# Routing words in cluster-major order, a pairwise maximum, and a DMA transpose in a fused attention and convolution kernel

## The chip, the cores and the metric

The kernel runs on one core of a Trainium2 chip. The engines that matter are TensorE (PE, matmul), VectorE (DVE), ScalarE (ACT), GpSimd (POOL) and SyncE (SP, which here only issues DMAs). The metric is the device time of one launch in microseconds; it is given as the median of several runs. Engines run side by side, each in its own instruction order, and wait for one another by semaphores.

## The reference

Every query and every key is assigned to one of 16 clusters (the first centroid of largest cosine), and a query attends only to keys of its own cluster. The attention output then goes through a gated long convolution.

```python
q_assign = np.argmax(np.einsum('bhsd,hcd->bhsc', q_n, c_n), axis=-1)
k_assign = np.argmax(np.einsum('bhsd,hcd->bhsc', k_n, c_n), axis=-1)
mask = q_assign[:, :, :, None] == k_assign[:, :, None, :]
scores = scale * np.matmul(q, k.transpose(0, 1, 3, 2))
scores = np.where(mask, scores, -1000000000.0)
...
proj = x @ w_proj
...
x2_conv = np.fft.irfft(X2 * H, n=S, axis=1)
y = x1 * x2_conv * x3
return (y @ w_out).astype(np.float32)
```

Sizes: batch 4, 8 heads, 768 tokens, head size 64, 16 clusters, model width 512.

## The kernel before

**Tiling.** The 32 heads are worked in eight groups (`n` = 0 to 7) of four heads; a group has two pairs of heads (`pr` = 0, 1). `attention(n, pr)` makes six steps over blocks of 128 keys. A step is three score products of 512 columns (L662, recorded as L70 or L72), three exponentials on ACT (L671, L674), one product with the values (L685) and a running sum of the exponentials on DVE (L699). After every second group `hyena(b)` adds the convolution of one batch element as filler work.

**The mask.** Cluster membership is not a separate step of the scores: it is 16 more rows of the contraction. The tile `aug` holds 64 rows of the head and 16 rows with a word for every token. For a key (`j` = 1) the word is one-hot; for a query (`j` = 0) it is 0 at its cluster and a large negative number elsewhere, so that a key of another cluster gets a score that the exponential turns to 0. There are three sets of `aug` tiles, used in turn (`ring`).

**Routing.** `routing(n)` makes these words for a whole group (4 heads, each with queries and keys, `z` counts pair and query/key). For groups 1 to 7 it goes so:

1. `sim` (L582): similarities of all tokens to the centroids on PE; copied out by ACT or DVE; transposed by PE (`simT`, L595), so that tokens lie on the 128 partitions and each partition has 48 words of 16 numbers.
2. DVE: the maximum of each word (L602), twice (two halves); a comparison with it (L604), twice. A word can now have several ones.
3. DVE: a product with the descending numbers `revc` (L607), a second maximum over all 48 words (L610) and a second comparison (L612), which leaves the first one of each word.
4. PE: six transposes of 128x128 back to words on partitions, each in two halves (`ohT`, L623), into a PSUM bank; ACT (or DVE) copies the bank to the tile `ohT` with a scale and an offset per partition, which makes the query's form of the word (L629, L631).
5. SP: eight small DMAs per group (`masks`, L459) carry 16 rows of `ohT` each to the `aug` tiles: first the four of `pr` = 0, then the four of `pr` = 1.

Group 0 has a path of its own (`first_masks`), pair by pair.

**Order.** `build` lists all operations with a cost per engine that may take them, and a due time. `Plan.place` is a list scheduler: at each step it takes, on the engine that comes free first, the operation of the smallest due time among those that are ready, with a few terms added: `bonus` favours staying with value products on PE, `shape` speaks against changing the width of the PE array, `BUSY` speaks against giving DVE an operation that another engine could take, `LEAD` is how far ahead of its due time a load may be issued. A DMA's landing is planned from its bytes, a rate and a constant (`done`). The result is one fixed instruction order for each engine. Due times hang on `A(i)`, the planned time of attention step `i` (`T0`, `TAU1` for the first 28 steps, `TAU2` after); the mask words of a group are due relative to `b0`, a fixed time ahead of the group's first score.

Of the kernel before, what the change touches and what calls it, by code (L numbers as in the profile page):

```python
# [32 lines left out]
NV = 3  # L33
NU = 4
ROWS = 16
LEAD = 0.305
FIRST = 2
BUSY = 1.562
HELD = 4
THIRDS = [[(0, 0, 512)], [(0, 512, 768), (1, 0, 256)], [(1, 256, 768)]]  # L40
HOLD = {"score": "score", "o": "o"}
# [33 lines left out]
class Plan:  # L75
# [31 lines left out]
        self.ops.append(o)  # L107
        return o

    def place(self, free0, banks_for, switch=0.1, wait=0.1, rate=215e3, bonus=8.964, margin=0.036, shape=2.605):  # L110
        free = dict(free0)
        bank_free = [0.0] * 8
        ready = {e: [] for e in free}
# [57 lines left out]
        while any(ready.values()):  # L171
            best = None
            for e, lst in ready.items():
                f = free[e]
                cand = []
                for o in lst:
                    t = max(f, o.ready)
# [22 lines left out]
            _, e, o, t = best  # L200
# [40 lines left out]
def build(T):  # L241

    P = Plan()
    op = P.op
    T0 = 12.859
    TAU1 = 3.281
    TAU2 = 3.567
    NE = 28

    def ring(n, pr):  # L250
# [2 lines left out]
    def A(i):  # L253
        return T0 + TAU1 * min(i, NE) + TAU2 * max(i - NE, 0)

# [8 lines left out]
    def ap(h):  # L264
        return bank(h.ids[0])

    def bank(i):
        return T.bank[i][:]
# [7 lines left out]
    def dma(e):  # L276
        return (T.nc.scalar if e == "ACT" else T.nc.sync).dma_start
# [174 lines left out]
    def masks(n, prs, due):  # L452
        out = []
        for pr in prs:
            a = ring(n, pr)
            for hp in range(2):
                for j in (1, 0):
                    r0 = 32 * (2 * pr + j) + 16 * hp
                    out.append(op(("SP", .6), lambda e, a=a, hp=hp, j=j, r0=r0: dma(e)(  # L459
                        T.augs[a][hp][j][64 - 64 * hp:80 - 64 * hp], T.ohT[r0:r0 + 16]), due + .3 * hp,  # L460
                        r=[("ohT", pr), ("zero", a, j)], w=[("augm", a, hp, j)], byts=25e3, lat=1.0))
        return out

# [70 lines left out]
    def routing(n):  # L534
# [38 lines left out]
                       w=[("aug", ring(n, pr), hp, j)], lock=True)  # L573
        if n == 0:
            return got + first_masks(1)
        b0 = end - 21.084
        h = Bank(cls, 2)

        def sim(e, h=h):
            for ch in range(2):  # L580
                for z in range(4):
                    T.nc.tensor.matmul(bank(h.ids[ch])[32 * z:32 * z + 32, :384], T.cbd[:, 2 * g + z // 2],  # L582
                                       T.qkT[z][:, ch], start=True, stop=True)
        op(("PE", 1.33), sim, b0, r=[("qkT", z, ch) for z in range(4) for ch in range(2)] + ["cbd"], w=[h], alloc=h,
           kind="sim")
# [12 lines left out]
        bc = lambda a: a.unsqueeze(len(a.shape)).to_broadcast([*a.shape, NC])  # L598
        flat = lambda: T.oh[:].rearrange("p a n c -> p (a n) c")
        for ch in range(2):  # L600
            sv = lambda ch=ch, h=h: bank(h.ids[ch])[:, :384].rearrange("p (n c) -> p n c", c=NC)
            op(("DVE", .55), lambda e, ch=ch, sv=sv: V().tensor_reduce(T.mx[:, ch], sv(), axis=AX, op=Alu.max),  # L602
               b0 + 3.3 + .2 * ch, r=[h], w=[("mx", ch)])
            op(("DVE", .55), lambda e, ch=ch, sv=sv: V().tensor_tensor(T.oh[:, ch], sv(), bc(T.mx[:, ch]),  # L604
                                                                       op=Alu.is_equal),
               b0 + 3.4 + .2 * ch, r=[h, ("mx", ch)], w=[("oh", ch)], free=[h])
        op(("DVE", .56), lambda e: V().tensor_tensor(  # L607
            flat(), flat(), T.revc[:].unsqueeze(1).to_broadcast([128, 48, NC]), op=Alu.mult), b0 + 4, r=["revc"],
           w=both("oh"), lock=True)
        op(("DVE", .96), lambda e: V().tensor_reduce(T.m2, T.oh, axis=AX, op=Alu.max), b0 + 4.1, r=both("oh"),  # L610
           w=both("m2"))
        op(("DVE", .97), lambda e: V().tensor_tensor(T.oh, T.oh, bc(T.m2[:]), op=Alu.is_equal), b0 + 4.2,  # L612
           r=both("m2"), w=both("oh"), lock=True)
        h = Bank(cls)
        due = b0 + 7.5

        def ohT(e, h=h):
            o = ap(h).bitcast(BF16)
            f = T.oh[:].rearrange("p a n c -> p (a n c)")
            for t in range(NT):  # L620
                for i in range(1 if T.whole else 2):
                    rs = slice(0, 128) if T.whole else slice(64 * i, 64 * i + 64)
                    T.nc.tensor.transpose(o[rs, ts(t, 128)], f[:, ts(t, 128)][:, rs], T.identb)  # L623
        op(("PE", .335), ohT, due, r=[("oh", 0), ("oh", 1), "identb"], w=[h], alloc=h, kind="proj")

        def rows(e, h=h):
            x = ap(h).bitcast(BF16)[:, :S]
            if e == "ACT":
                T.nc.scalar.activation(T.ohT, x, Act.Identity, scale=T.mka, bias=T.mkb)  # L629
            else:  # L630
                T.nc.vector.tensor_scalar(T.ohT, x, T.mka, T.mkb, op0=Alu.mult, op1=Alu.add)  # L631
        op({"ACT": .83, "DVE": .68}, rows, due + .5,
           r=[h, "mk"], w=[("ohT", 0), ("ohT", 1)], free=[h])
        masks(n, range(2), due + 1.3)


# [308 lines left out]
    def constants():  # L945
        G = lambda: T.nc.gpsimd

        def ident(e):
            make_identity(T.nc, T.ident)
        op(("POOL", 1.0), ident, 0, w=["ident"])  # L950

        def iotas(e):
            kw = dict(allow_small_or_imprecise_dtypes=True)
            G().iota(T.s0t, pattern=[[2, 3]], base=0, channel_multiplier=6, **kw)
            for i in range(2):
                G().iota(T.kc[:, i], pattern=[[2, 192]], base=i, channel_multiplier=0, **kw)
            G().memset(T.kc[:, 0, 0:1], float(HS))
        op(("POOL", .8), iotas, .0, w=["kc", "s0t0"])

        def freqs(e):  # L960
            kw = dict(allow_small_or_imprecise_dtypes=True)
            G().iota(T.kp[:, :2], pattern=[[1, 2]], base=0, channel_multiplier=2, **kw)
            G().iota(T.kp[:, 2:], pattern=[[0, 1]], base=256, channel_multiplier=2, **kw)
        op(("POOL", .3), freqs, 3.5, w=["kp0"])
        op(("DVE", .15), lambda e: T.nc.vector.tensor_scalar(T.kp[64:, 2:], T.kp[64:, 2:], -127.0, None, op0=Alu.add), 4,
           r=["kp0"], w=["kp"])

        def half(e):
            for i in range(2):
                h = T.s0t[64 * i:64 * i + 64]  # L970
                T.nc.vector.tensor_scalar(h, h, 0.5 - 383.0 * i, None, op0=Alu.add)
            T.nc.vector.tensor_scalar(T.s1t, T.s0t, 1.0 / S, None, op0=Alu.mult)
        op(("DVE", .5), half, .3, r=["s0t0"], w=["s0t", "s1t"])

        def small(e):
            G().memset(T.cbd, 0.0)
            G().memset(T.half_pi, math.pi / 2)
            for g in range(4):
                G().memset(T.mka[32 * g:32 * g + 32], BIG if g % 2 == 0 else 1.0)
                G().memset(T.mkb[32 * g:32 * g + 32], -BIG if g % 2 == 0 else 0.0)  # L980
            G().iota(T.revc, pattern=[[-1, NC]], base=NC, channel_multiplier=0, allow_small_or_imprecise_dtypes=True)
        op(("POOL", .9), small, .4, w=["cbd0", "half_pi", "mk", "revc"])
# [89 lines left out]
def kernel(  # L1072
# [34 lines left out]
    T.half_pi, T.warm = col("half_pi"), col("warm")  # L1107
    T.mka, T.mkb = (col(x) for x in ("mka", "mkb"))
    T.revc, T.mx, T.m2 = tl([128, NC], BF16, "revc"), tl([128, 2, 24], F32, "mx"), tl([128, 2, 24], BF16, "m2")
    T.qkraw = [tl([128, NT, 2, D], F32, f"qkraw{i}") for i in range(NQK)]  # L1110
    T.vraw = [tl([128, 2, 384], F32, f"vraw{i}") for i in range(NV)]
    T.augs = [[[tl([128, S], BF16, f"aug{i}{hp}{j}") for j in range(2)] for hp in range(2)] for i in range(3)]
# [61 lines left out]
```

The softmax here doesn't subtract the row's maximum and nothing guards it: scores larger than these inputs give would overflow.

## Time and profile before

| | before |
|---|---|
| median of 8 runs | 396.07 us (394.41 to 397.56) |
| the profiled execution's own time | 395.23 us |
| its span, first to last instruction | 393.4 us |
| DVE busy | 358.4 us (91%) |
| ACT busy | 271.4 us (69%) |
| POOL busy | 45.0 us (11%) |
| granted TensorE clock | 0.999 |
| DMA | 45.81 MB, mean 116 GB/s |

The span lacks 1.8 us of the execution's own time; the median of the runs is 0.84 us above that execution. "Busy" is the time in which an engine has an instruction running, with the ends of matmuls modelled, so a busy PE can still hold short waits. A row of instructions reads: line, engine, operation, output from input, number; busy time and mean of one; idle time of that engine just before them and what ended it.

### The profile page before, as it was taken

The numbers are of one execution on the slowest core, as the hardware profiler recorded it, in microseconds if no ns is written. First come the engines' busy times: TensorE is split into PE (matmuls) and PEld (weight loads), VectorE is DVE, ScalarE is ACT, GpSimd is POOL, SyncE is SP. The second block draws the span as 40 slices with busy tenths as digits, with TensorE's granted clock in tenths as the row PEclk, the third lists the DMA queues.
The fourth block names the chain that finished last, engine by engine and source line by source line (L and its number), as shares of the span: only waits on it lengthen the run. The fifth ranks groups of instructions, "written<-read, shape, count | busy, mean of one in ns | idle before, by whom it ended". The sixth has DMA issues, their size and how long they took to land.

```text
span 393.4 us, 8641 instructions
## 1 busy us (share of the span) xinstructions
PE 373.4 (95%) x3355; PEld 214.3 (54%) x3358; DVE 358.4 (91%) x491; ACT 271.4 (69%) x512; POOL 45.0 (11%) x89
## 2 busy tenths in 40 slices
PE   3988989999999999999999999999999999999994
PEld 2553445455545545555554555656555677655672
DVE  8897879989979999999999999899998999999782
ACT  5997688988875769777868468778956467532342
POOL 8400100000002100101010100101010100000400
PEclk9999999999999999999999999999999999999999
DMA  9919957333487856664856775734646541010214
GB/s 178 225 28 211 218 133 169 84 85 74 109 198 108 120 121 108 131 127 66 198 95 182 124 211 85 168 36 67 123 58 179 109 113 38 15 35 2 109 56 160
DMA packets 88261, 45.81 MB, mean 116 GB/s; under 512 B 76488, under 2 KB 82076, under 8 KB 88220
## 3 DMA queue, kind: packets, MB, share of 16 engines
q1 hardware_dynamic: 82236, 35.46, 38.4%
q0 software_dynamic: 2704, 8.98, 15.5%
q10 hardware_dynamic: 3280, 0.82, 1.2%
q8 instruction: 26, 0.43, 0.5%
q14 instruction: 15, 0.12, 0.1%
HBM read 31.59 MB, written 7.40 MB: 99 GB/s over the span
## 4 chain that ended last, share of the span: by engine, by line
PE 68%; DVE 19%; issue 5%; DMA 4%; ACT 3%; ACTq 0%; SPq 0%; POOL 0%; DVEq 0%; POOLq 0%
PE bank L72 25%; PE pair L685 24%; DVE acc L699 6%; PE bank L811 4%; PE bank L70 4%; PE bank L553 3%; PE bank L582 2%; ACT p L674 2%; PE bank L448 1%; PE bank L713 1%; DMA dr<-dn 1%; DMA rb<-dr 1%; DVE tm L835 1%; DVE yy L910 1%; DVE aug L260 1%
## 5 line engine op out<-in xcount | busy, mean ns | idle before, releaser
L685 PE MATMUL pair<-p,vraw 128*64 128x385 f32 x768 | 145.4, 490 | 1.3 <-DVE inv L260 1.3
L674 ACT ACTIVATE p<-bank 128x512 f32<-128x512 f32 x192 | 114.6, 612 | 39.3 <-PE bank L72 34.7
L699 DVE TENSOR_TENSOR acc<-p,acc 128x1536 f32<-128x1536 f32 x64 | 112.0, 1749 | 2.8 <-ACT p L674 1.0
L685 PEld LDWEIGHTS pair<-p,vraw 128*64 128x64 f32 x768 | 57.7, 136 | 50.9 <-issue 39.9
L72 PE MATMUL bank<-aug,aug 80*64 80x512 bf16 (+3 forms) x544 | 72.8, 328 | 1.2 <-DVE hm L435 1.1
L671 ACT ACTIVATE p<-bank 128x512 f32<-128x512 f32 x96 | 58.3, 607 | 14.1 <-PE bank L72 12.4
L733 POOL DMA_DIRECT2D acc<-acc x30 | 23.8, 793 | 247.2 <-DVE acc L699 90.4
L72 PEld LDWEIGHTS <-aug 80*64 80x64 bf16 (+1 forms) x544 | 35.2, 109 | 29.7 <-issue 22.1
L72 PE MATMUL bank<-xT,wpj 128*64 128x384 bf16 x456 | 46.7, 326 | 0.2 <-DVE sd L900 0.2
L258 ACT COPY qkT<-bank 128x384 f32<-128x384 f32 x60 | 27.6, 499 | 12.6 <-PE bank L72 9.2
L72 PEld LDWEIGHTS <-wpj 128*64 128x64 bf16 x456 | 28.3, 109 | 14.4 <-issue 5.6
L72 PEld LDWEIGHTS <-y 128*64 128x64 bf16 x480 | 25.1, 110 | 10.6 <-issue 2.6
L699 DVE TENSOR_TENSOR acc<-p,p 128x1536 f32<-128x1536 f32 x16 | 28.0, 1753 | 2.3 <-ACT p L674 2.2
L835 DVE TENSOR_TENSOR tm<-bank,hm 128x512 f32<-128x512 f32 x44 | 27.8, 677 | 1.4 <-POOL y L839 0.8
L70 PE MATMUL bank<-aug,aug 80*128 80x512 bf16 (+3 forms) x111 | 25.6, 321 | 3.2 <-DMA aug<-ohT 0.8
L258 ACT CAST aug<-qkT 64x768 bf16<-64x768 f32 x30 | 24.9, 829 | 0.5
L811 PE MATMUL bank<-wpj,xT 128*64 128x512 bf16 x192 | 22.9, 379 | 0.0
L72 PE MATMUL bank<-wout,y 128*64 128x512 bf16 x160 | 21.3, 379 | 0.0
L703 ACT COPY osb<-pair 128x770 f32<-128x770 f32 x16 | 13.0, 812 | 11.4 <-PE pair L685 11.2
L553 PEld LDWEIGHTS bank<-ident,qkraw 128*128 128x128 f32 x144 | 15.6, 140 | 8.8 <-issue 3.0
L553 PE MATMUL bank<-ident,qkraw 128*128 128x128 f32 x144 | 20.3, 279 | 0.0
L260 DVE CAST aug<-qkT 64x768 bf16<-64x768 f32 x31 | 17.4, 568 | 0.4
(151 smaller groups left out, 442.1 us busy)
## 6 DMA issues: line engine op xcount, KB each, us to landing
vraw<-in_v_dram SPq DMA_DIRECT2D x16, 384.0 KB, 3.7
qkraw<-in_q_dram SPq DMA_DIRECT2D x30, 192.0 KB, 3.7
qkraw<-in_k_dram SPq DMA_DIRECT2D x30, 192.0 KB, 4.3
rb<-dr SPq DMA_DIRECT2D x30, 192.0 KB, 3.2
out_dram<-ob SPq DMA_DIRECT2D x11, 512.0 KB, 4.1
acc<-acc POOLq DMA_DIRECT2D x10, 384.0 KB, 4.7
acc<-acc POOLq DMA_DIRECT2D x10, 192.0 KB, 4.3
y<-in_moe_filter_fft_dram SPq DMA_DIRECT2D x4, 384.0 KB, 8.1
```

Source lines behind the costliest of these rows:

```text
L70: return T.nc.tensor.matmul(out, lhsT, rhs, start=start, stop=stop)
L72: T.nc.tensor.matmul(out[64 * i:64 * i + 64], lhsT[:, 64 * i:64 * i + 64], rhs, start=start, stop=stop)
L258: T.nc.scalar.copy(out, in_)
L260: (T.nc.vector if e == "DVE" else T.nc.gpsimd).tensor_copy(out, in_)
L553: T.nc.tensor.transpose(bank(h.ids[i // 3])[:, ts(i % 3, 128)], raw(s, i), T.ident)
L671: T.nc.scalar.activation(o, ap(h).rearrange("p (a b) -> p a b", a=2), Act.Exp, scale=0.125)
L674: T.nc.scalar.activation(flat(s)[:, lo:lo + 512], ap(h), Act.Exp, scale=0.125)
L685: T.nc.tensor.matmul(o[64 * hp:64 * hp + 64, ch, :385], T.vraw[vs][:, hp, sk * D:(sk + 1) * D], T.p[slots[sk]][:, hp, 384 * ch:384 * ch + ...
L699: T.nc.vector.tensor_tensor(T.acc[os], P_(t[0]), P_(t[1]) if len(t) == 2 else T.acc[os], op=Alu.add)
L733: op(("POOL", .8), lambda e, rows=rows: T.nc.gpsimd.dma_start(flat_()[:rows], flat_()[rows:2 * rows], accum_op=Alu.add), te, r=[], w=[("ac ...
L811: T.nc.tensor.matmul(ap(h)[64 * i:64 * i + 64], T.xT[xs][:, kt, c:c + 64], T.wpj[:, kt, DM:2 * DM], start=kt == 0, stop=kt == ND - 1)
L835: op(("DVE", .68), lambda e, i=i, cs=cs, r=r, h=h: T.nc.vector.tensor_tensor(T.tm[r][:, cs], ap(h), hmrow(i, (0, 2, 2, 3)[2 * r + cs]), op ...
```

## The change

The tile of words changes its order from (word, cluster) to (block of four words, cluster, word in the block): the 128 columns that one block transposes then hold, for four words, cluster 0 of each, cluster 1 of each, and so on. The `sim` product writes its four results to other partitions, so that keys come to one half and queries to the other after the transpose. The product with the descending numbers uses `revx`, the same numbers repeated four times and scaled by 262144 in advance. The second maximum is no longer one reduction but four maxima of pairs (8, 4, 2 and 1 clusters remain) in the scratch tile `mt`. The second comparison is split: keys keep the comparison, queries subtract the maximum, which gives the 0 and the large negative numbers at once. The six PE transposes and the copy with scale and offset are replaced by one DMA transpose on SP, which writes `ohT` directly. The eight DMAs of `masks` read every fourth row. Group 0 keeps its path. The constants of the order (`LEAD`, `BUSY`, `bonus`, `margin`, `shape`, `T0`, `TAU1`, `TAU2`, the distance of `b0`, the window of `hyena`) have new values.

```diff
-LEAD = 0.305
+LEAD = 1.92382
-BUSY = 1.562
+BUSY = 8.22961
...
-    def place(self, free0, banks_for, switch=0.1, wait=0.1, rate=215e3, bonus=8.964, margin=0.036, shape=2.605):
+    def place(self, free0, banks_for, switch=0.1, wait=0.1, rate=215e3, bonus=9.59846, margin=0.01958, shape=1.54891):
...
-    T0 = 12.859
-    TAU1 = 3.281
-    TAU2 = 3.567
+    T0 = 20.32396
+    TAU1 = 2.98503
+    TAU2 = 3.43812
...
-                    r0 = 32 * (2 * pr + j) + 16 * hp
+                    rows = slice(64 * j + 2 * pr + hp, 64 * j + 64, 4) if n else slice(64 * pr + 32 * j + 16 * hp, 64 * pr + 32 * j + 16 * hp + 16)
...
-        b0 = end - 21.084
+        b0 = end - 24.00720
...
-                    T.nc.tensor.matmul(bank(h.ids[ch])[32 * z:32 * z + 32, :384], T.cbd[:, 2 * g + z // 2],
+                    T.nc.tensor.matmul(bank(h.ids[ch])[64 * (z % 2) + 32 * (z // 2):][:32, :384], T.cbd[:, 2 * g + z // 2],
...
-        op(("DVE", .96), lambda e: V().tensor_reduce(T.m2, T.oh, axis=AX, op=Alu.max), b0 + 4.1, r=both("oh"),
-           w=both("m2"))
-        op(("DVE", .97), lambda e: V().tensor_tensor(T.oh, T.oh, bc(T.m2[:]), op=Alu.is_equal), b0 + 4.2,
-           r=both("m2"), w=both("oh"), lock=True)
+        def largest(e):
+            x = words()
+            for n_ in (8, 4, 2, 1):
+                y = T.mt[:, 48 * n_ - 48:96 * n_ - 48].rearrange("p (m c i) -> p m c i", m=12, c=n_)
+                V().tensor_tensor(y, x[:, :, :n_], x[:, :, n_:], op=Alu.max)
+                x = y
+        op(("DVE", .85), largest, b0 + 4.1, r=both("oh"), w=both("m2"), lock=True)
+        for j, o_ in ((1, Alu.is_equal), (0, Alu.subtract)):
+            op(("DVE", .36), lambda e, j=j, o_=o_: V().tensor_tensor(
+                words()[:, j::2], words()[:, j::2],
+                T.mt[:, :48].rearrange("p (m i) -> p m i", i=4)[:, j::2].unsqueeze(2).to_broadcast([128, 6, NC, 4]), op=o_),
+               b0 + 4.2, r=both("m2"), w=both("oh"), lock=True)
         due = b0 + 7.5
-        op(("PE", .335), ohT, due, r=[("oh", 0), ("oh", 1), "identb"], w=[h], alloc=h, kind="proj")
-        op({"ACT": .83, "DVE": .68}, rows, due + .5,
-           r=[h, "mk"], w=[("ohT", 0), ("ohT", 1)], free=[h])
+        op(("SP", .6), lambda e: T.nc.sync.dma_start_transpose(
+            T.ohT[:].rearrange("p (t n) -> p t n", n=128), T.oh[:].rearrange("p a n c -> p (a n c)")), due - 2,
+           r=both("oh"), w=both("ohT"), byts=196e3, lat=1.0)
         masks(n, range(2), due + 1.3)
...
-        w0 = A(24 * (b + 1)) + 26.258
-        w1 = A(24 * (b + 2)) + 51.473 if b < B - 2 else A(96) + 22.054
+        w0 = A(24 * (b + 1)) + 11.88829
+        w1 = A(24 * (b + 2)) + 50.54365 if b < B - 2 else A(96) + 33.48240
         if last:
-            w0 = A(96) - 3.814
+            w0 = A(96) - 0.31306
...
+            G().iota(T.revx, pattern=[[-1, NC], [0, 4]], base=NC, channel_multiplier=0, **kw)
+            G().tensor_scalar(T.revx, T.revx, BIG, None, op0=Alu.mult)
```

More of the change, by code (lines that the diff above doesn't have):

```diff
@@ L457, in masks @@
                 for j in (1, 0):
-                    r0 = 32 * (2 * pr + j) + 16 * hp
-                    out.append(op(("SP", .6), lambda e, a=a, hp=hp, j=j, r0=r0: dma(e)(
-                        T.augs[a][hp][j][64 - 64 * hp:80 - 64 * hp], T.ohT[r0:r0 + 16]), due + .3 * hp,
+                    rows = slice(64 * j + 2 * pr + hp, 64 * j + 64, 4) if n else slice(64 * pr + 32 * j + 16 * hp, 64 * pr + 32 * j + 16 * hp + 16)
+                    out.append(op(("SP", .6), lambda e, a=a, hp=hp, j=j, rows=rows: dma(e)(
+                        T.augs[a][hp][j][64 - 64 * hp:80 - 64 * hp], T.ohT[rows]), due + .3 * hp,
                         r=[("ohT", pr), ("zero", a, j)], w=[("augm", a, hp, j)], byts=25e3, lat=1.0))
@@ L597, in routing @@
         op(("PE", .68), simT, b0 + 2.5, r=SIM + ["ident"], w=[h], alloc=h)
-        bc = lambda a: a.unsqueeze(len(a.shape)).to_broadcast([*a.shape, NC])
-        flat = lambda: T.oh[:].rearrange("p a n c -> p (a n) c")
+        words = lambda: T.oh[:].rearrange("p a n c -> p (a n c)").rearrange("p (m c i) -> p m c i", c=NC, i=4)
         for ch in range(2):
-            sv = lambda ch=ch, h=h: bank(h.ids[ch])[:, :384].rearrange("p (n c) -> p n c", c=NC)
-            op(("DVE", .55), lambda e, ch=ch, sv=sv: V().tensor_reduce(T.mx[:, ch], sv(), axis=AX, op=Alu.max),
+            sv = lambda ch=ch, h=h: bank(h.ids[ch])[:, :384].rearrange("p (m i c) -> p m i c", i=4, c=NC)
+            mx = lambda ch=ch: T.mx[:, ch].rearrange("p (m i) -> p m i", i=4)
+            op(("DVE", .55), lambda e, sv=sv, mx=mx: V().tensor_reduce(mx(), sv(), axis=AX, op=Alu.max),
@@ L603, in routing @@
                b0 + 3.3 + .2 * ch, r=[h], w=[("mx", ch)])
-            op(("DVE", .55), lambda e, ch=ch, sv=sv: V().tensor_tensor(T.oh[:, ch], sv(), bc(T.mx[:, ch]),
-                                                                       op=Alu.is_equal),
-               b0 + 3.4 + .2 * ch, r=[h, ("mx", ch)], w=[("oh", ch)], free=[h])
+            op(("DVE", .55), lambda e, ch=ch, sv=sv, mx=mx: V().tensor_tensor(
+                words()[:, 6 * ch:6 * ch + 6].rearrange("p m c i -> p m i c"), sv(), mx().unsqueeze(3).to_broadcast([128, 6, 4, NC]),
+                op=Alu.is_equal), b0 + 3.4 + .2 * ch, r=[h, ("mx", ch)], w=[("oh", ch)], free=[h])
@@ L607, in routing @@
         op(("DVE", .56), lambda e: V().tensor_tensor(
-            flat(), flat(), T.revc[:].unsqueeze(1).to_broadcast([128, 48, NC]), op=Alu.mult), b0 + 4, r=["revc"],
+            words(), words(), T.revx[:].unsqueeze(1).to_broadcast([128, 12, NC, 4]), op=Alu.mult), b0 + 4, r=["revx"],
            w=both("oh"), lock=True)
-        op(("DVE", .96), lambda e: V().tensor_reduce(T.m2, T.oh, axis=AX, op=Alu.max), b0 + 4.1, r=both("oh"),
-           w=both("m2"))
-        op(("DVE", .97), lambda e: V().tensor_tensor(T.oh, T.oh, bc(T.m2[:]), op=Alu.is_equal), b0 + 4.2,
-           r=both("m2"), w=both("oh"), lock=True)
@@ L614, in routing @@
-        h = Bank(cls)
-        due = b0 + 7.5
[L617 to L623, printed above, removed]
-        op(("PE", .335), ohT, due, r=[("oh", 0), ("oh", 1), "identb"], w=[h], alloc=h, kind="proj")
@@ L626, in rows @@
[L626 to L631, printed above, removed]
-        op({"ACT": .83, "DVE": .68}, rows, due + .5,
-           r=[h, "mk"], w=[("ohT", 0), ("ohT", 1)], free=[h])
+        def largest(e):
[4 more added lines that the diff above has]
+                x = y
@@ L980, in small @@
                 G().memset(T.mkb[32 * g:32 * g + 32], -BIG if g % 2 == 0 else 0.0)
-            G().iota(T.revc, pattern=[[-1, NC]], base=NC, channel_multiplier=0, allow_small_or_imprecise_dtypes=True)
-        op(("POOL", .9), small, .4, w=["cbd0", "half_pi", "mk", "revc"])
+            kw = dict(allow_small_or_imprecise_dtypes=True)
+            G().iota(T.revc, pattern=[[-1, NC]], base=NC, channel_multiplier=0, **kw)
+            G().iota(T.revx, pattern=[[-1, NC], [0, 4]], base=NC, channel_multiplier=0, **kw)
+            G().tensor_scalar(T.revx, T.revx, BIG, None, op0=Alu.mult)
+        op(("POOL", .9), small, .4, w=["cbd0", "half_pi", "mk", "revc", "revx"])
         op(("DVE", .3), lambda e: T.nc.vector.tensor_copy(T.identb, T.ident), 3, r=["ident"], w=["identb"])
@@ L1109 @@
     T.revc, T.mx, T.m2 = tl([128, NC], BF16, "revc"), tl([128, 2, 24], F32, "mx"), tl([128, 2, 24], BF16, "m2")
+    T.revx, T.mt = tl([128, NC, 4], BF16, "revx"), tl([128, 720], BF16, "mt")
     T.qkraw = [tl([128, NT, 2, D], F32, f"qkraw{i}") for i in range(NQK)]
```

## Prediction, written before the result was known

> **What bounds the kernel.** I read the page first (busy shares, chain of waits), then sums by stage, then the rows of the routing step, then the timeline around one group's masks.
>
> ```profile
> PE 373.4 (95%) x3355; PEld 214.3 (54%) x3358; DVE 358.4 (91%) x491; ACT 271.4 (69%) x512; POOL 45.0 (11%) x89
> ...
> PE 68%; DVE 19%; issue 5%; DMA 4%; ACT 3%; ACTq 0%; SPq 0%; POOL 0%; DVEq 0%; POOLq 0%
> ```
>
> PE carries 68% of the chain that ended last, DVE 19%. By stages (window; PE, PEld, DVE, ACT and POOL busy):
>
> ```profile
> 30.00:60.00 30.00, 27.32 (x217) 12.87 (x217) 23.09 (x30) 21.83 (x38) 2.60 (x5) 1.00 0.89 181
> 60.00:110.00 50.00, 49.85 (x404) 26.11 (x403) 46.21 (x46) 42.26 (x83) 0.00 (x0) 1.00 0.46 109
> 110.00:170.00 60.00, 59.22 (x498) 32.04 (x492) 57.37 (x76) 41.71 (x78) 8.03 (x10) 1.00 0.71 131
> 170.00:240.00 70.00, 69.51 (x592) 37.49 (x590) 68.69 (x94) 52.09 (x98) 7.07 (x9) 1.00 0.69 141
> 240.00:300.00 60.00, 58.70 (x544) 34.47 (x538) 57.25 (x77) 45.43 (x86) 7.17 (x9) 1.00 0.53 97
> ```
>
> From 60 us on PE has next to no gap, and from 110 to 300 DVE is at 183.3 of 190 us. So PE work taken out shortens the span, DVE work taken out helps a little, ACT work (69%) only as room for other work. What is added must not make PE, which runs a fixed order, wait.
>
> **The change, part by part.** Groups 1 to 7 change. The rows of the tile of words before (columns: number; minimum, median, maximum in ns):
>
> ```profile
> L623 PE MATMUL bank<-identb,oh x84: 217/219/243, 50.1 to 288.6; 128*64 128x128 bf16 x84
> ...
> L604 DVE TENSOR_TENSOR oh<-bank,mx x14: 496/546/549, 44.8 to 284.9; 128x384 bf16<-128x384 f32 x14
> L607 DVE TENSOR_TENSOR oh<-oh,revc x7: 558/559/560, 45.9 to 285.5; 128x768 bf16<-128x768 bf16 x7
> L610 DVE TENSOR_REDUCE m<-oh x7: 943/953/955, 46.5 to 286.1; 128x48 bf16<-128x768 bf16 x7
> L612 DVE TENSOR_TENSOR oh<-oh,m x7: 957/957/959, 47.5 to 287.1; 128x768 bf16<-128x768 bf16 x7
> ...
> L494 DVE TENSOR_TENSOR oh<-oh,revc x2: 357/358/358, 17.1 to 21.4; 128x384 bf16<-128x384 bf16 x2
> ```
>
> *PE.* The 84 half transposes overlap; summed by window they keep PE busy 3.57 us, 0.51 a group. They go: -3.6 us on the path. (Counted from start to start of the next matmul they are about 2.5 us; I keep 3.6 and use 2.5 for the range.) `sim` and `simT` keep their numbers of matmuls.
>
> *DVE.* Two rows of one operation give its law: 384 numbers 358 ns, 768 numbers 559 ns, so 157 ns plus 0.52 ns a number. The tree writes 384, 192, 96 and 48: 358 + 257 + 207 + 182 = 1.00 us, against 0.95 for the reduction. Each half of the second comparison is 384 numbers. Its broadcast operand now has four neighbours in a row, which the broadcast of L612 (957 ns for 768) had not, so I take L494's 0.36: two make 0.72 against 0.96. L602, L604 and L607 keep sizes; L604 now writes with a stride of four, for which no row stands near, and I leave 0.55. Sum: 2.28 against 2.47, -0.19 a group, -1.3 in all; with DVE 19% of the chain, -0.3 us. The other end: if these short inner runs get L612's rate (157 + 1.04 a number), tree and comparisons take 2.5 us, +0.6 a group, +4 us of DVE, of which 19% to all would reach the end.
>
> Here a rule speaks on the tree: the Trainium skill (VectorE: DVE Perf Modes, errata section) prices an SBUF operation at 58 cycles plus the numbers over the mode's factor, which makes the tree 4 x 60 ns + 720 x 0.52 = 0.62 us, a gain of 0.33 a group over the reduction. The rows' fixed 157 ns says the four starts eat that. The rows decide.
>
> *ACT.* Seven copies of `ohT` at 0.99 us go, 6.9 us. ACT isn't the bound: it waits 34.7 us and 12.4 us for scores (L674, L671). Nothing by itself. The larger `BUSY` will move copies from DVE to ACT: L260 has 31 casts of `aug` at 0.57 us on DVE (17.4 us), which cost ACT 0.83 each (L258). If all moved, ACT would have 271 - 7 + 26 = 290 us, still under PE.
>
> *The DMA transpose.* It is new to the trace, so its landing must be bounded. The nearest rows, issue to landing:
>
> ```profile
> qkraw<-in_q_dram SPq DMA_DIRECT2D x30, 192.0 KB, 3.7
> ...
> rb<-dr SPq DMA_DIRECT2D x30, 192.0 KB, 3.2
> ...
> aug<-ohT SPq DMA_DIRECT2D x60, 24.0 KB, 3.1
> ...
> dp<-dd SPq DMA_DIRECT2D x10, 96.0 KB, 2.8
> ...
> dr<-dn SPq DMA_DIRECT2D x15, 6.0 KB, 1.9
> ```
>
> Equal bytes land in 3.2 to 3.7 us: the low end. A transpose moves small pieces, and `dp` is the row with small ones: 48 bytes each, so 2,048 of them, cost 0.9 us over the 1.9 us of a tiny DMA. At pieces of 32 bytes (my assumption) 192 KB are 6,144, so 1.9 + 2.7 = 4.6 us. I take 4.6. The rule that speaks against: the same page (section on the three transpose paths) gives 1,309 ns for one 128x128 bf16 block by DMA and 390 ns by TensorE. If six blocks add up, the landing is 7.9 us, or 9.8 us with the 1.9 us of a small DMA on top. (By its TensorE figure the six would be 2.3 us of PE; the trace has 0.51 because they overlap, so the page overstates what is removed, too.) Taken together: low end 3.2, high end 9.8, value 4.6, nearest to `dp`.
>
> How much can the masks bear? Group 2:
>
> ```profile
> 83.61 0.96 DVE L612 TENSOR_TENSOR oh<-oh,m 128x768 bf16<-128x768 bf16 x1
> ...
> 85.58 0.99 ACT L629 ACTIVATE ohT<-bank,mkb,mka 128x768 bf16<-128x768 bf16 x1
> ...
> 86.59 1.89 SPq L459 DMA_DIRECT2D aug<-ohT  x2
> ...
> 89.21 3.67 SPq L459 DMA_DIRECT2D aug<-ohT  x6
> ...
> 94.03 0.97 PEld L70 LDWEIGHTS <-aug 80*128 80x128 bf16 x7
> ```
>
> Words done at 84.6, first score with them at 94.0: 9.5 us. In the same way the other groups have 9.6 to 11.3 us. Behind the transpose come four mask issues (three steps of 0.6 us) and 3.1 us to landing: 4.9 us. The change also begins routing 24.0 instead of 21.1 us ahead of the group's first score, 2.9 us more. So the transpose may take 9.5 + 2.9 - 4.9 = 7.5 us before PE waits. At 4.6 us it is covered, by attention steps of the group before; without the 2.9 us it would be just at the edge (4.6). PE's waits on masks before (0.8 us) then go: -0.8 us.
>
> *SP's queue.* Per group one more DMA, which waits for DVE, and behind it the mask DMAs wait for its landing; before, they waited for ACT. What stands behind them on SP is the chain of the row sums (`dn<-dd`, `dr<-dn`, `rb<-dr`, L727 to L750) and the next loads (L292). `rb` is read on DVE by L779, which waits 1.6 us in all, and only `hyena` needs that result. The planner's own sum for this DMA is 0.6 + 1.3 + 0.9 + 0.6 + 1.0 = 4.4 us, so what it slips in between fits 4.6.
>
> *Start.* Two more POOL operations after the `iota` of L981 (0.20 us): some 0.4 us ahead of the zeroing of `aug`; POOL's first dependent cast has 0.57 us of idle ahead of it, which covers them; without that cover, 0.4 us.
>
> *New due times.* A new order for all engines. It can't be added up from rows. PE's gap from 40 to 345 us is 305 - 300.55 = 4.4 us, and another 4.5 us lie between 10 and 60 us: that is all the visible idle it could close, and short waits inside "busy" besides. It can as well open gaps: attention is asked to run 5% faster (28 steps of 3.28 and 68 of 3.57 us become 2.99 and 3.44) with DVE already at 96%. I take 0, from -8 to +8.
>
> *Sum*: -3.6 - 0.3 - 0.8 = -4.7 us on the profiled execution's 395.23, so 390.5; the median of the runs stands 0.84 us above it: **391.4 us**.
>
> **Rivals.**
>
> *Late transpose* (slower). One mechanism: blocks of the DMA transpose run one after another, landing at 9.8 us against the 7.5 that the masks can bear. PE stands at the first score of each group for 2.3 us, 7 times, 16 us: 391.4 + 16 = 407 us. It decides from 7.5 us upward. For: small pieces, no such row in the trace, the page's 1,309 ns. Against: rows of equal size at 3.2 to 3.7.
>
> *Worse order* (slower). PE's and DVE's new order doesn't fit their real times: DVE stays at its limit, copies pushed to ACT come between exponentials and hold up scores. I price it by the +8: 399 us. For: DVE 96%, ACT up to 290 us. Against: PE is still the longest engine.
>
> *Better order.* The relief of DVE by casts closes gaps: 391.4 - 6 = 385 us.
>
> *No net effect.* The new waits eat the 4.7 us: 396 us.
>
> **Numbers.** About 0.3% is what a measurement tells from no change here. Forecast (388 to 394.8) 0.42, better order 0.10, no net effect 0.10, worse order 0.20, late transpose 0.18. So faster 0.52, same 0.10, slower 0.38. Range 384 to 406: it leaves out the late transpose from 406 up (0.13) and some of the better order (0.04). The likeliest case alone is 388 to 394.8.
>
> **What would show it.** No L623 and L629 rows in groups 1 to 7; the tree near 1.0 us and the two comparisons near 0.36 each; the transpose's landing (under 7.5 us: covered); PE's waits "aug<-ohT" under 1 us; PE busy down to about 370 us; fewer casts of `aug` on DVE. I am wrong if PE shows waits of over 2 us at the first score of each group, or if its busy time rises.

## The result and the profile after

| | before | after |
|---|---|---|
| median | 395.59 us (33 runs, 394.41 to 397.56) | 393.07 us (12 runs, 390.62 to 394.65) |
| ratio, 95% interval | | 0.993 (0.9914 to 0.9947) |
| the profiled execution, its span | 395.23 us, 393.4 us | 394.65 us, 392.9 us |

The change is faster by 2.5 us, about half of the 4.7 us that were forecast. Executions more than 1.5% above the fastest of the same kernel are left out of medians and ratios, which concerns only two of the runs below, with two planned and with three transposes. The profiled execution of after is the longest of its 12, so the two traces differ by 0.6 us only; where a trace is read below, it is read for what takes how long, and times are compared by medians.

Busy shares and the chain of waits of the kernel after:

```profile
PE 369.4 (94%) x3233; PEld 208.6 (53%) x3238; DVE 359.4 (91%) x509; ACT 271.8 (69%) x515; POOL 46.3 (12%) x91
...
PE 50%; DVE 31%; issue 8%; DMA 4%; ACT 4%; SPq 1%; ACTq 0%; DVEq 0%; POOL 0%; POOLq 0%
```

PE has lost 4.0 us of busy time (373.4 to 369.4), about what the transposes made (3.6). DVE has not lost anything: 358.4 has become 359.4, and its part of the chain went from 19% to 31%. The rows of the words alone add 5.4 us to DVE; the new order took 4.4 us of other work off it, mostly copies out of PSUM that went to ACT (DVE copies `sim` once where it did 4 times, `x` once for 3, `ob` once for 3). So ACT got back what it lost with the copies of `ohT`: 271.4 us have become 271.8. The same stages as before (window; PE, PEld, DVE, ACT and POOL busy):

```profile
110.00:170.00 60.00, 57.47 (x484) 31.78 (x481) 57.62 (x81) 41.29 (x78) 7.12 (x9) 1.00 0.75 130
170.00:240.00 70.00, 67.14 (x539) 37.49 (x542) 65.84 (x92) 52.32 (x98) 7.05 (x9) 1.00 0.78 148
240.00:300.00 60.00, 58.20 (x502) 33.08 (x500) 57.65 (x83) 46.03 (x88) 7.05 (x9) 1.00 0.57 98
```

From 110 to 300 us PE is busy 182.8 us where it was 187.4: it now has gaps in the middle, 7.2 us in these 190 where they were 2.6. The work went, and part of its time became waiting. The rows of the words tell one reason (number; minimum, median, maximum in ns):

```profile
L605 DVE TENSOR_TENSOR oh<-bank,mx x14: 940/1022/1067, 38.5 to 284.7; 128x384 bf16<-128x384 f32 x14
L620 DVE TENSOR_TENSOR oh<-oh,mt x14: 351/354/361, 45.5 to 288.1; 128x384 bf16<-128x384 bf16 x14
L608 DVE TENSOR_TENSOR oh<-oh,revx x7: 535/557/559, 40.4 to 286.1; 128x768 bf16<-128x768 bf16 x7
L616 DVE TENSOR_TENSOR mt<-oh x7: 357/358/359, 41.0 to 286.7; 128x384 bf16<-128x384 bf16 x7
L625 SPq DMA_TRANSPOSE ohT<-oh x7: 1272/1382/1777, 50.6 to 288.5; - x7
```

The first comparison (L605, L604 before) takes 1,022 ns in place of 546, 14 times: 6.7 us more on DVE. It is the instruction that now writes its 2-byte results 8 bytes apart. The rest of the step is as worked out: the second comparison 0.35 us a half, the tree 1.01 us by its four means (358 + 258 + 208 + 184). The DMA transpose costs SP 1.38 us to issue. The landings of two of the seven are told apart, 2.8 and 3.6 us after the issue; in the other groups the first mask, which waits for the landing, goes out 2.9 to 5.2 us after the issue.

### The profile page after: what moved, and what is told of

The parts are those of the page before. It is cut to its first block, busy times and chain, and to the rows that moved or that the text cites. A ratio compares the mean times of both kernels' runs of the same rounds, so it can differ in the third digit from the quotient of the medians.

```text
span 392.9 us, 8460 instructions
## 1 busy us (share of the span) xinstructions
PE 369.4 (94%) x3233; PEld 208.6 (53%) x3238; DVE 359.4 (91%) x509; ACT 271.8 (69%) x515; POOL 46.3 (12%) x91
## 4 chain that ended last, share of the span: by engine, by line
PE 50%; DVE 31%; issue 8%; DMA 4%; ACT 4%; SPq 1%; ACTq 0%; DVEq 0%; POOL 0%; POOLq 0%
PE bank L72 18%; PE pair L679 14%; DVE acc L693 11%; PE bank L70 5%; PE bank L805 5%; PE bank L553 3%; DVE oh L605 3%; DMA rb<-dr 2%; DVE aug L260 2%; DMA aug<-ohT 1%; DVE x L869 1%; PE bank L448 1%; ACT aug L258 1%; DVE xT L773 1%; DVE mx L603 1%
## 5 line engine op out<-in xcount | busy, mean ns | idle before, releaser
L679 PE MATMUL pair<-p,vraw 128*64 128x385 f32 x768 | 142.6, 490 | 0.0
L679 PEld LDWEIGHTS pair<-p,vraw 128*64 128x64 f32 x768 | 54.5, 136 | 47.9 <-issue 42.3
L72 PE MATMUL bank<-aug,aug 80*64 80x512 bf16 (+3 forms) x578 | 69.5, 327 | 5.2 <-DVE tm L829 1.6
L72 PE MATMUL bank<-xT,wpj 128*64 128x384 bf16 x416 | 40.8, 326 | 1.5 <-DVE oh L605 1.5
L72 PEld LDWEIGHTS <-wpj 128*64 128x64 bf16 x416 | 24.7, 109 | 16.2 <-issue 8.4
L72 PEld LDWEIGHTS <-y 128*64 128x64 bf16 x432 | 21.8, 110 | 11.8 <-issue 3.3
L805 PE MATMUL bank<-wpj,xT 128*64 128x512 bf16 x192 | 22.0, 380 | 0.1
L70 PE MATMUL bank<-aug,aug 128*128 128x256 bf16 (+3 forms) x93 | 20.2, 322 | 0.2 <-DVE aug L517 0.2
L553 PE MATMUL bank<-ident,qkraw 128*128 128x128 f32 x144 | 19.4, 279 | 0.2 <-DVE oh L605 0.2
L260 DVE CAST aug<-qkT 64x768 bf16<-64x768 f32 x32 | 18.2, 568 | 1.3 <-PE bank L72 0.8
```

The costliest lines, as they stand in the source:

```text
L70: return T.nc.tensor.matmul(out, lhsT, rhs, start=start, stop=stop)
L72: T.nc.tensor.matmul(out[64 * i:64 * i + 64], lhsT[:, 64 * i:64 * i + 64], rhs, start=start, stop=stop)
L260: (T.nc.vector if e == "DVE" else T.nc.gpsimd).tensor_copy(out, in_)
L679: T.nc.tensor.matmul(o[64 * hp:64 * hp + 64, ch, :385], T.vraw[vs][:, hp, sk * D:(sk + 1) * D], T.p[slots[sk]][:, hp, 384 * ch:384 * ch + ...
L805: T.nc.tensor.matmul(ap(h)[64 * i:64 * i + 64], T.xT[xs][:, kt, c:c + 64], T.wpj[:, kt, DM:2 * DM], start=kt == 0, stop=kt == ND - 1)
```

## The experiments

Each starts from the kernel named; "new order" is the set of constants of the changed kernel, "old order" that of the kernel before.

### One access turned round

```diff
-                words()[:, 6 * ch:6 * ch + 6].rearrange("p m c i -> p m i c"), sv(), mx().unsqueeze(3).to_broadcast([128, 6, 4, NC]),
+                words()[:, 6 * ch:6 * ch + 6], sv().rearrange("p m i c -> p m c i"), mx().unsqueeze(2).to_broadcast([128, 6, NC, 4]),
```

> The changed kernel with one edit: the first comparison writes its words in the order of memory and reads PSUM with a stride, in place of reading PSUM in order and writing 2-byte numbers 8 bytes apart. Theory 'strided write': the comparison's 1.02 us (before: 0.55) is the price of the strided write; here it returns to about 0.55 us, DVE busy falls from 359.4 to about 353 us, and the time falls from 393.1 to 390 to 391.5 us. Rival 'strided anything': a strided read of PSUM costs the same, the comparison stays near 1.0 us and the time near 393. Rival 'DVE is covered': the comparison gets shorter, but the time stays within 1 us of 393.

Measured: 388.89 us, ratio to before 0.9833 (0.9793 to 0.9873). The row of the comparison, and the engines' busy times:

```profile
L605 DVE TENSOR_TENSOR oh<-bank,mx x14: 496/546/557, 37.9 to 280.6; 128x384 bf16<-128x384 f32 x14
```

```profile
PE 368.7 (95%) x3233; PEld 210.5 (54%) x3238; DVE 353.9 (91%) x509; ACT 271.4 (70%) x515; POOL 46.2 (12%) x91
```

The same numbers compared in the same order of instructions, only walked along the output instead of along the input: 546 ns again. So the strided write was the price, and here the strided read of PSUM has none. 5.5 us less on DVE made the kernel 4.2 us shorter (1.7 us to either side, by the intervals of the two ratios). This version is ahead of both kernels.

### Is it DVE's queue, or the path to the masks?

The comparison lies on the path to the masks, so the gain could come from masks that are ready 1 us sooner. This run puts a useless reduction on DVE behind each group's words:

```diff
+                j or V().tensor_reduce(T.m2, T.oh, axis=AX, op=Alu.max)),
```

> The kernel with the strided read (388.89 us) and, behind the last step of each group's words, one more reduction of 0.95 us on DVE whose result nobody reads: 6.7 us of DVE work off the path to the masks, about what the strided read saved on that path. Theory 'DVE's queue is the limit': it costs what the strided write did, 392 to 394 us. Rival 'the path to the masks is the limit': the strided read won because each group's masks came 1 us sooner; this work lies behind them, and the time stays at 388.5 to 390.5 us.

Measured: 392.83 us (ratio 0.9941, 0.9923 to 0.996). Its row, of the tile of words:

```profile
L623 DVE TENSOR_REDUCE m<-oh x7: 952/953/954, 44.0 to 287.7; 128x48 bf16<-128x768 bf16 x7
```

DVE busy goes from 353.9 to 360.2 us, and the time from 388.89 to 392.83. In the trace the transpose does not wait for this reduction: in group 2 the words end at 79.64, the transpose is issued and the reduction starts at 79.67. Work off the path to the masks costs nearly what the strided write cost on it: it is DVE's queue. A us of DVE is worth 3.9 / 6.3 = 0.63 us here, and 4.2 / 5.5 = 0.76 us in the run above, each with about 0.3 to either side.

### A us of PE

In the kernel before, each group's transposes made twice:

```diff
-            for t in range(NT):
+            for t in [*range(NT)] * 2:
```

> The kernel before in its own order, with the six PE transposes of each group made twice (the second writes the same numbers to the same bank). Theory 'PE work counts in full': 84 half transposes more are 3.6 us by busy time, 2.5 us from start to start; the time goes from 395.7 to 398.2 to 399.3 us. Rival 'PE has cover here': under 1 us more.

Measured: 397.19 us against 395.91, ratio 1.0032 (1.002 to 1.0044). Its engines:

```profile
PE 376.0 (95%) x3442; PEld 220.1 (56%) x3442; DVE 359.0 (91%) x491; ACT 271.2 (69%) x512; POOL 45.2 (11%) x89
```

2.6 us more of busy PE cost 1.3 us (0.8 to 1.7). So these matmuls count for half: between the theories, nearer to cover than to the full price. (They were added to the kernel before, not taken from it; that a us taken out is worth the same is assumed.) PE at 95% busy wasn't the harder limit of the two.

### How much delay the masks bear

The changed kernel, the transpose issued twice, and three times, in its own order:

```diff
-        op(("SP", .6), lambda e: T.nc.sync.dma_start_transpose(
-            T.ohT[:].rearrange("p (t n) -> p t n", n=128), T.oh[:].rearrange("p a n c -> p (a n c)")), due - 2,
+        op(("SP", .6), lambda e: [T.nc.sync.dma_start_transpose(
+            T.ohT[:].rearrange("p (t n) -> p t n", n=128), T.oh[:].rearrange("p a n c -> p (a n c)")) for _ in range(2)], due - 2,
```

> The changed kernel in its own order; each DMA transpose is issued twice in a row into the same tile, so that the masks start later by one issue and landing (1.4 us if the second does not wait for the first, 3.2 us if it does). Theory of the prediction (the masks bear a landing of 7.5 us): 4.6 to 6.5 us are still covered, time 392.5 to 395 us. Rival 'no slack left': the masks already make PE wait, every us of delay costs up to 7 us, 402 us and more.

> As the run with two, three transposes in a row; landing 6 us (no wait between) to 9.7 us (each waits). Theory of the prediction: over 7.5 us PE stands at each group's first score, (9.7 - 7.5) x 7 = 15 us more than the changed kernel, 408 us; if it lands at 6 us, no loss, 393 to 395. Rival 'no slack left': 415 us and more.

Measured: twice 416.15 us (ratio 1.0514, 1.0478 to 1.055); three times 430.6 us in the fastest of four runs and 438.2 to 444.6 in the others, too scattered for a ratio. By the number the rival is right. The traces say otherwise of its reason. The two spans differ by 19.1 us (392.9 and 412.0). PE's busy time with two transposes:

```profile
PE 377.6 (92%) x3238; PEld 211.4 (51%) x3238; DVE 360.2 (87%) x509; ACT 271.9 (66%) x515; POOL 46.5 (11%) x91
```

It is 8.2 us longer than in the changed kernel, for the same matmuls: in this trace PE ran four times at half its clock before the last value product, 17 us in all. The rest is standing. Who waited for the tile `ohT` in the changed kernel, and with two transposes (total us, times):

```profile
  PEld L72: 3.3, 2
  PE bank L72: 0.8, 2
  PEld bank L553: 0.6, 1
```

```profile
  PEld L72: 10.6, 7
  PE bank L72: 8.9, 6
  PE bank L70: 1.9, 1
```

So PE's own waits on masks grew from 0.8 to 10.8 us (a weight load, PEld, often waits in the same gap). The second transpose waits for the first, and the delay that it makes is not one number. From the end of the words to the first mask on SP, by group, and PE's waits on masks with two transposes:

| group | first mask after the words, changed kernel | with two transposes | PE then waits |
|---|---|---|---|
| 1 | 7.8 | 10.6 | 2.0 |
| 2 | 3.8 | 6.1 | 0 |
| 3 | 2.9 | 13.3 | 3.5 |
| 4 | 4.8 | 7.2 | 2.1 |
| 5 | 5.2 | 10.3 | 0 |
| 6 | 4.3 | 9.1 | 2.2 |
| 7 | 3.6 | 7.7 | 1.0 |

The masks came 2.3 to 10.4 us later, 32 us in all. The expectations had put the delay at 1.4 to 3.2 us, so this run does not try what they speak of; why the second transpose lands so late in some groups (9.5 us after its issue in group 3) is not shown. Group 6 in the changed kernel, then with two transposes:

```profile
248.74 1.78 SPq L625 DMA_TRANSPOSE ohT<-oh  x1
...
253.05 4.39 SPq L459 DMA_DIRECT2D aug<-ohT  x7
```

```profile
262.58 5.57 SPq L625 DMA_TRANSPOSE ohT<-oh  x2
...
271.66 4.97 SPq L459 DMA_DIRECT2D aug<-ohT  x8
...
274.91 0.41 PE L72 MATMUL bank<-aug,aug 80*64 80x512 bf16 x2 [2.16 <-DMA aug<-ohT]
```

Where the first mask goes out 6.1 us after the words, PE does not stand; from 7.2 us upward it does, except in group 5. So the masks do bear a delay. In group 5 the first score comes late for another reason: there the longest gap of this trace, 4.17 us, is for the row sums. Their DMA `rb` stands on SP behind both transposes, DVE waits for it, and PE for DVE:

```profile
219.18 1.18 SPq L744 DMA_DIRECT2D rb<-dr  x2
...
223.62 1.02 DVE L773 SCALAR_TENSOR_TENSOR xT<-osb,rb 128x768 bf16<-128x768 f32 x1 [4.09 <-DMA rb<-dr]
...
224.69 1.92 PE L805 MATMUL bank<-wpj,xT 128*64 128x512 bf16 x8 [4.17 <-DVE xT L773]
```

Group 2 of the changed kernel (SP's and PE's timeline):

```profile
81.45 1.30 SPq L625 DMA_TRANSPOSE ohT<-oh  x1
82.80 0.59 SPq L292 DMA_DIRECT2D qkraw<-in_k_dram  x1
83.49 0.58 SPq L298 DMA_DIRECT2D vraw<-in_v_dram  x1
84.58 0.57 SPq L719 DMA_DIRECT2D dd<-den  x1
85.20 5.65 SPq L459 DMA_DIRECT2D aug<-ohT  x8
...
92.05 0.39 PE L72 MATMUL bank<-aug,aug 80*64 80x512 bf16 x2
```

The words are done at 81.4. The transpose lands at 84.3 (2.8 us), and three other DMAs that the plan had put into the wait are issued, before the first mask goes out at 85.2; the first score stands at 92.0. With two transposes the masks of this group went out 2.3 us later against the words, and the first score did not move: it has 10.6 us in both traces.

**The order told of it.** If the two transposes are known to the plan, does the loss go?

```diff
-        op(("SP", .6), lambda e: [T.nc.sync.dma_start_transpose(
+        op(("SP", 3.6), lambda e: [T.nc.sync.dma_start_transpose(
```

> The changed kernel with two transposes in a row (416 us unplanned), and the order drawn up with that delay in it (3.0 us more on SP for this operation). Theory 'mismatch with the order': the 23 us came from a landing that the fixed order did not know; told of it, the order puts other work there and most of it is recovered, below 402 us. Rival 'the latency itself': the masks are on the path whatever the order, 408 us and more.

Measured: 412.1 us (1.042, 1.0388 to 1.0453), which is what the rival said. Neither theory is shown by it: PE's own waits on masks did fall, from 10.8 to 3.5 us in the traces, but the order is another one altogether, and, as the next runs show, another order alone can cost that much.

### The step and its order apart

> The new routing step with all due times and weights of the kernel before. Theory 'the step pays': less PE work is worth its 2 to 3 us whatever the order, time 393 to 394.5 us. Rival 'the order pays': the gain of the changed kernel is its new order, and the step alone, with DVE 4 us longer and masks 2 us later, gives 395.5 to 398 us, with PE waiting for masks for over 5 us in all.

> The old routing step with the due times and weights of the changed kernel. Theory 'the step pays': no gain from the order, 395 to 398 us. Rival 'the order pays': 392 to 394 us.

> The changed kernel with the DMA transpose put back to six PE transposes and a copy out of PSUM (without scale and offset). Theory 'PE work counts in full': PE busy is 3.6 us longer, ACT 6.9 us longer, time 395.5 to 397 us. Rival 'the transpose's landing costs as much as it saves': within 1 us of the changed kernel, 392 to 394 us, with PE's waits on masks gone.

> The new routing step with the due times of before (403.95 us) and with the first comparison writing in order of memory and reading with a stride. Theory 'DVE work': the same 5.5 us of DVE go as in the new order, and the time falls by 4 to 6 us, to 398 to 400 us. Rival 'order': 404 is a matter of the order alone (its tail has gaps of PE), the edit gives less than 2 us, 402 to 404. If it falls below 395, the step pays in the old order, too.

> The kernel with the strided read, with two costs of its plan set to what the trace shows (tree 1.0 in place of 0.85 us, issue of the transpose 1.4 in place of 0.6 us). If the remaining waits on masks (about 5 us by PE's rows) come from the plan being short there, they shrink and the time falls by 1 to 3 us, 386 to 388; if a new order matters more than its truth, it lands anywhere from 386 to 400 us.

The edits are the constants of the diff above, in both directions; for the run with PE transposes the operations `ohT` and its copy are put back in place of the DMA; for the one with true costs:

```diff
-        op(("DVE", .85), largest, b0 + 4.1, r=both("oh"), w=both("m2"), lock=True)
+        op(("DVE", 1.0), largest, b0 + 4.1, r=both("oh"), w=both("m2"), lock=True)
...
-        op(("SP", .6), lambda e: T.nc.sync.dma_start_transpose(
+        op(("SP", 1.4), lambda e: T.nc.sync.dma_start_transpose(
```

| kernel | time us | ratio to before (95%) | last value product starts at | PE from there to its end | PE gaps in that tail |
|---|---|---|---|---|---|
| before | 395.59 | | 347.4 | 40.6 | 0.2 |
| after | 393.07 | 0.993 (0.9914 to 0.9947) | 345.4 | 42.5 | 0.7 |
| after, strided read | 388.89 | 0.9833 (0.9793 to 0.9873) | 341.2 | 42.5 | 0.7 |
| new step, old order | 403.95 | 1.0219 (1.0199 to 1.024) | 349.9 | 45.7 | 4.1 |
| the same, strided read | 399.99 | 1.01 (1.0075 to 1.0126) | 348.1 | 45.7 | 4.1 |
| old step, new order | 397.27 | 1.0031 (1.0016 to 1.0046) | 335.8 | 51.8 | 5.9 |
| after, PE transposes | 407.45 | 1.0294 (1.0274 to 1.0315) | 342.3 | 56.2 | 9.5 |
| strided read, true costs | 402.22 | 1.0177 (1.0152 to 1.0202) | 339.8 | 54.6 | 7.5 |
| two transposes, planned | 412.1 | 1.042 (1.0388 to 1.0453) | 349.5 | 52.3 | 6.6 |

(The last three columns are from one trace each; "tail" is what follows the last value product.) Three things follow. The strided read gives 4.0 us in the old order, too: about what it gave in the new one. Neither half of the change pays alone: the step without its order loses 8.2 us, the order without its step 1.5 (against 395.74 us for before on the same chip). The 8.2 us are not the masks: where the expectation had PE wait over 5 us for them, its trace has 0.2 us. And in every kernel whose order was drawn up by constants made for another one, the tail is longer than the changed kernel's 42.5 us, by 3 to 14 us, with 4 to 10 us of PE gaps in it, while attention ends within 3 us of before, or sooner. The runs with PE transposes and with true costs therefore say little on their own questions. With true costs two small numbers in the plan were made right, and the kernel lost 13 us.

In the run with true costs the same work follows the last value product as with the strided read alone: 519 matmuls there, 507 here, of which 12 over the whole array each do the work of two. Its stages there, and then those of the strided read with its old costs (window; PE, PEld, DVE, ACT and POOL busy; then the granted clock):

```profile
360.00:365.00 5.00, 2.02 (x26) 1.51 (x22) 5.00 (x10) 0.96 (x2) 3.41 (x3) 0.92 0.00 0
365.00:370.00 5.00, 4.25 (x52) 3.91 (x54) 3.89 (x7) 0.48 (x1) 0.00 (x0) 0.50 0.01 3
370.00:375.00 5.00, 5.00 (x82) 4.18 (x78) 1.67 (x4) 1.92 (x4) 0.00 (x0) 0.90 0.00 0
```

```profile
360.00:365.00 5.00, 5.00 (x58) 3.19 (x56) 5.00 (x10) 1.95 (x4) 3.42 (x3) 1.00 0.01 2
365.00:370.00 5.00, 5.00 (x82) 3.69 (x80) 2.33 (x5) 1.99 (x5) 0.00 (x0) 1.00 0.54 213
370.00:375.00 5.00, 5.00 (x88) 4.14 (x86) 4.69 (x9) 2.74 (x6) 0.00 (x0) 1.00 0.28 108
```

DVE is full while PE stands, 3.55 us by PE's timeline, for the sum `y` of the last batch element (L833); and around the end of the gap PE falls to half its clock.

### The transpose of group 1 first

One gap of this kind is in the best version: at 58.4 us PE stood 2.06 us for the masks of group 1. On SP alone, two loads were put behind the transpose:

```diff
+    at = next(i for i, o in enumerate(order) if o.kind == "turn")
+    late = [o for o in order[:at] if o.on == "SP" and o.kind == "load"][-2:]
+    order = [o for o in order[:at] if o not in late] + [order[at]] + late + order[at + 1:]
```

> The kernel with the strided read (388.89 us); on SP alone, the transpose of group 1 is put ahead of the two loads of qkraw that stood in front of it (in the profile the first of them held SP from 40.9 to 48.8 us, while the words were done at 44.6 and the transpose was issued at 50.0; PE then stood 2.06 us for the masks of group 1 and its granted clock was halved for the 3.4 us after). Theory 'the loads hold SP by a wait of their own': the transpose is issued at about 44.7 us, masks follow by 52, PE's 2.06 us gap and the half clock go, time 385 to 387.5 us. Rival 'the DMA queue is full': whatever DMA stands there is held up as long, the masks come no sooner, time 388 to 390 us.

Measured: 389.16 us (0.9824, 0.9794 to 0.9855), no gain over 388.89. SP's timeline with the strided read, then with the transpose first:

```profile
40.93 9.00 SPq L292 DMA_DIRECT2D qkraw<-in_k_dram  x2
50.03 1.35 SPq L625 DMA_TRANSPOSE ohT<-oh  x1
...
55.32 5.01 SPq L459 DMA_DIRECT2D aug<-ohT  x8
```

```profile
45.32 5.19 SPq L625 DMA_TRANSPOSE ohT<-oh  x1
50.62 1.25 SPq L292 DMA_DIRECT2D qkraw<-in_k_dram  x2
...
53.40 5.94 SPq L459 DMA_DIRECT2D aug<-ohT  x8
```

The transpose is issued when the words are done, and now it is the one that is held, 5.2 us in place of 1.35, so it is not the loads' own wait. That a full queue holds them, as the rival has it, is not shown; and the masks do come 1.9 us sooner. The gap of 2.06 us is gone in this trace, and with it the half clock, but the median is no shorter. The runs of the strided read differ by their clock: the shortest, 386.6 us, had 1.000 on average, the profiled one, 390.5 us, 0.992. So what its trace lost there wasn't lost in every run, and whether the edit is worth anything stays open.

## Why the prediction was half right

**Direction and time.** Forecast 391.4, measured 393.07; the likeliest case's own range (388 to 394.8) holds it. The mechanism is seen: no transposes and copies, PE busy down by 4.0 us (forecast 3.6), the second comparison at 0.35 (0.36), the tree at 1.01 (1.00). The row of the trace was right on the tree, and the estimate of 0.62 us from the table of the Trainium skill (VectorE: DVE Perf Modes, errata section) was not; that section says below its table that the measured fixed term is about 150 cycles rather than 58, and four of these would have made it 1.0 us. The hit is in part luck: at the prices measured below, PE, DVE and masks make -1.3 us where the sum had -4.7, all three too good, and -1.2 us from no known cause brought the time back toward the forecast.

**The term that was mis-sized.** "L604 now writes with a stride of four, for which no row stands near, and I leave 0.55": it is 1.02. The DVE sum of the routing step for a group is not 2.28 against 2.47; with both comparisons it grows by 0.96 - 0.19 = 0.77 us, 5.4 us in all. An unknown was entered at its low end with no high end. Nor did the casts of `aug` leave DVE (31 before, 32 after); copies out of PSUM left in their place. The Trainium skill has a sentence on it (SBUF — State Buffer, "Door 1: The DMA port swizzle"): 8 bf16 numbers can be stepped over free of charge. That would give 0.55 here, and the trace disagrees: a step of 4 bf16 numbers in DVE's write made 546 ns 1,022. That is 1.24 ns more for each of the 384 numbers, more than the 1.0 ns that one takes without the step (an estimate, with the 157 ns of the other rows as the fixed part: (546 - 157) / 384).

**The weights.** PE was counted in full and DVE at its 19% of the chain. The runs give about a half for PE (1.3 us for 2.6) and 0.63 to 0.76 for DVE. The stage sums had it on the page: DVE at 183 of 190 us beside PE at 187 is not a helper; two engines stood at their limit, and the chain names only the one that ended last at each step.

**The masks' slack.** The landing was taken as 4.6 us, and 2.8 to 5.2 us are seen; but the reason given for it does not hold. It rested on 6,144 pieces of 32 bytes, and the two pages differ by 5,599 packets and 1.36 MB, some 240 bytes each. The 7.5 us that the masks were said to bear fit the run with two transposes roughly (no wait at 6.1 us, waits from 7.2 us upward), by two errors that cancel. "Words done at 84.6, first score with them at 94.0" takes the second score product of the step for the first, which is this one of the kernel before:

```profile
90.88 0.38 PE L72 MATMUL bank<-aug,aug 80*64 80x512 bf16 x1
```

It has the masks 6.3 us after the words, not 9.5. Counted by the exponentials (36 a group, of which the traces have all 288), the seven groups have from words to first score 6.0 to 9.7 us before (mean 7.7) and 9.0 to 16.9 us after (mean 12.1). So the new order gave 4.4 us more on average, not the "2.9 us more" of the due time, from a base that was smaller: 12.4 us by the prediction, 12.1 measured. The rival of a late transpose did not come true because the transpose landed in 5.2 us or less. Its price, seven times the excess, leaves out two things that the run with two transposes shows: the row sums behind the transpose on SP, and PE's slower clock after a wait. The waits on masks did not go (-0.8 us): PE's row has 0.8 us as before, its weight loads 3.9 us (3.3 and 0.6) where they had 2.1.

**The order.** Taken as 0 with 8 us to both sides. The new constants with the old step cost 1.5 us, the old constants with the new step 8.2. How much of the 2.5 us is the step's and how much the order's stays open: with 0.5 for PE and 0.7 for DVE the two busy times (-4.0 and +1.0) make -1.3 us, and the other -1.2 us was not traced to a cause. By the same prices (an estimate) the 5.4 us of DVE that the step adds outweigh the PE work that it saves; that the plan, drawn up anew, took 4.4 us of other work off DVE turns the sum.

## What to carry to other kernels

Where two engines are each over 90% busy in a stage, the chain's shares do not price their work: here it was worth about 0.5 of its time on PE and 0.6 to 0.8 on DVE. An access pattern for which no row exists is an unknown with a high end: choose the side to stride on by a trial, here the read of PSUM and not the write of 2-byte numbers. In a fixed order, look at everything that stands behind a new DMA on its queue, not only at what waits for its result. Constants tuned for one step can lose more with another than the step wins: compare variants of a step in one order, by edits that the plan does not see.

## What was not expected of the hardware

A PE gap of 2.06 us was followed by half the clock for 3.4 us. The strided read in that stretch, and the same windows with the transpose first, where the largest gap was 0.45 us:

```profile
58.00:62.00 4.00, 1.94 (x24) 0.90 (x20) 1.90 (x2) 1.85 (x4) 0.00 (x0) 0.99 0.11 32
62.00:65.00 3.00, 3.00 (x20) 1.25 (x14) 2.49 (x6) 2.99 (x6) 0.00 (x0) 0.50 0.11 19
```

```profile
58.00:62.00 4.00, 3.31 (x35) 1.44 (x32) 3.16 (x4) 3.42 (x7) 0.00 (x0) 1.00 0.09 26
62.00:65.00 3.00, 2.55 (x22) 1.25 (x18) 2.91 (x5) 2.57 (x6) 0.00 (x0) 1.00 0.41 89
```

So a wait can be paid twice, once as a gap and once as slow matmuls behind it that read as busy. The length of the gap alone does not settle it. With two transposes a gap of 2.00 us before 61.80 left the clock full (first fence), and with the strided read in the old order two gaps of 0.69 and 0.97 us before 65.53 were followed by 3.4 us of half clock (second fence):

```profile
60.00:62.00 2.00, 0.20 (x4) 0.30 (x6) 1.51 (x1) 0.32 (x1) 0.00 (x0) 1.00 0.11 38
62.00:65.00 3.00, 3.00 (x32) 1.38 (x30) 0.98 (x3) 2.86 (x6) 0.00 (x0) 1.00 0.06 10
```

```profile
63.00:66.00 3.00, 1.34 (x8) 0.54 (x6) 3.00 (x5) 2.94 (x6) 0.00 (x0) 0.99 0.33 125
66.00:69.00 3.00, 3.00 (x15) 0.67 (x14) 1.31 (x3) 2.28 (x5) 0.00 (x0) 0.50 1.19 230
```

What decides is not shown. And a DMA issue is not a fixed cost: one issue held SP for 7.8 us (the first of the two loads at 40.93), where 0.6 us is usual; what held it is not shown either.
